# Gated attention and a square-plus MLP on one core: another order of some 1,000 pieces of work, and two of the last four stores issued by ScalarE

## The chip, the cores and the metric

The kernel runs on one core of a Trainium2 chip. Its time is the device time of one execution in microseconds. A core has five engines with an instruction queue each: TensorE (PE, with a weight load PEld ahead of each matmul), VectorE (DVE), ScalarE (ACT), GpSimd (POOL) and SyncE (SP), and 16 DMA engines that all DMAs share, whichever engine issues them. Each engine works through its own queue in order; semaphores order the engines among each other.

## The reference

Inputs `q`, `k`, `v`, `f_logit` have the shape (4, 8, 768, 48): 4 batches, 8 heads, 768 tokens, 48 channels. `w_in` is 384 x 2048 and `w_out` 2048 x 384, all fp32.

```python
f = 1.0 / (1.0 + np.exp(-f_logit))
for t in range(S):
    state = f[:, :, t, :, None] * state + np.einsum('bhd,bhe->bhde', k[:, :, t], v[:, :, t])
    y[:, :, t] = np.einsum('bhd,bhde->bhe', q[:, :, t], state)
...
x = y.transpose(0, 2, 1, 3).reshape(B * S, H * D)      # 3072 x 384
h = x @ w_in
g = 0.5 * (h + np.sqrt(h * h + 4.0))
return (g @ w_out).astype(np.float32)                  # 3072 x 384
```

## The kernel before

**Strips.** The 3072 tokens are cut into 12 strips of 256 tokens, p = 0 to 11; three strips make a batch, so strips 0, 3, 6 and 9 begin with an empty state. A strip is two chunks of 128 tokens (cc = 0, 1). The recurrence is done in blocks: within a chunk as a masked product of scaled q and k, between chunks through a state that is handed on. Strip 0 is loaded and prepared in two halves of four heads (`FINE = [0]`), the others whole.

**Pieces.** `describe` makes a table of named pieces of work; each is a function that emits a few instructions. Nothing is emitted there. The string `ORDER` lists all pieces, one word each, `name:engine` with the PSUM banks behind `@`, and the kernel's last loop walks through it and emits them. The place in the string is the place in that engine's queue: D is VectorE, P is POOL, A ScalarE, S SP, T TensorE. So each engine's queue is written out by hand (or by a program that wrote the string), and an instruction whose input is late holds everything listed behind it on its engine. `cost`, `lock`, `mode` and the like in the table belong to the program that finds an order; the chip doesn't see them.

**The pieces of a strip p**, by the names in the string:
- `lf`, `lk`, `lq`, `lv`: the loads of f, k, q, v, fp32, issued by SP (L174), each into one of three buffers, so that strip p waits until strip p-3 has used its own.
- `ex` (exp of -f, ACT), `ut` (adds 1, DVE), `tt` (product of a pair of tokens), `ln` (ACT), `hi` and `lo` (the logarithm split in two fp16 parts), `cu` (its running sum, on PE), `c1` (DVE), `ep` and `ea` (exp of plus and minus the sum, ACT), `ge`, `gs`, `gb` (the chunk's decay factors).
- `qu`, `ku`, `qm`, `km`: q and k scaled with these; most are on POOL, at 1 and 2 us each.
- `tp` and `te` (strips 0 to 3: transposes of the scaled q and k on PE, copied out of PSUM) or `tx` (strips 4 to 11: DMA transposes, two for a strip, issued by SP, L373).
- `vc`: v cast to fp16. `sc`: scores on PE (L414), `pm`: the mask (DVE). `kv`: the chunk's own state (L442); `ia`, `sp`, `sa`, `sb`: the state added, scaled and handed on. `yt` and `yn`: y from inside the chunk and from the state (L492, L501); `yc`: y copied out of PSUM.
- `xp` and `xe` (strips 0 to 3) or `xx` (strips 4 to 11, a DMA transpose issued by SP, L516): x transposed for the MLP.
- `m1.p.0` to `m1.p.7`: h, six matmuls of 256 columns each (L541); `sq` (square, ACT, L550), `rt` (square root of a pair, ACT, L556), `gt` (g, DVE, L566).
- `m2.p.00` to `m2.p.13`: the output of chunk cc in four quarters (L578), four matmuls of 384 columns each; a quarter n needs the weights `wo`n. `ev`: copied out of PSUM into one of two output buffers `os` (DVE or ACT). `st`: the stores, two for a strip, one for each half of the partitions; for strip 11, whose output leaves chunk by chunk (`SPLIT_OUT`), four. All are issued by SP (L598). `ev` of strip p waits until both stores of strip p-2 have landed.
- `wi0` to `wi3`, `wo0` to `wo3`: the weights of the MLP, in four parts each, issued by POOL with a cast to fp16 (L148, L153). `m1.p.m` needs `wi`(m // 2).
- `TABLE:e` and `TABLE:s` load ScalarE's table for exp and logarithm or for the square root.

The order is a software pipeline: the MLP of strips p-1 and p-2 fills PE while strip p's attention is prepared on the other engines. Around the start, the loads of strips 0 and 1 and the chain `ex`, `ut`, `tt`, `ln`, `hi`, `lo`, `cu` stand first. At the end only the MLP of strips 8 to 11 is left. The end of the string:

```python
m2.10.03:T gt11.6:D m2.11.02:T ev10.0:D m2.11.10:T@5 st10.01.1:S m2.11.11:T st10.01.0:S m2.11.03:T m2.11.12:T ev11.0:D
m2.11.13:T st11.0.0:S st11.0.1:S ev11.1:A st11.1.0:S st11.1.1:S
```

and SP's words around strip 10's transposes, without the other engines':

```python
xx8:S st5.01.0:S tx10.0:S st5.01.1:S tx10.1:S tx11.0:S xx9:S tx11.1:S st6.01.0:S
```

Of the kernel before, what the change touches and what calls it, by code (L numbers as in the profile page):

```python
# [28 lines left out]
DEPTH = {'f': 3, 'q': 3, 'k': 3, 'v': 3, 'UT': 3, 's': 2, 'ep': 2, 'ea': 2, 'v16': 4, 'ge': 3, 'gs': 4, 'gb': 3, 'qkT0': 2, 'qkT1': 2, 'pm00': 2, 'pm01': 2, 'pm10': 2, 'pm11': 2, 'st0': 1, 'pc': 4, 'st1': 1, 'sn0': 2, 'sn1': 2, 'y16': 2, 'xT': 5, 'hsq': 3, 'r16': 3, 'g': 4, 'os': 2}  # L29

ORDER = """
lf0.1:S lf0.0:S lf1.0:S lk0.0:S lk0.1:S TABLE:e ex0.1:A lq0.1:S ut0.1:D ex0.0:A lq0.0:S tt0.1:P ut0.0:D ln0.1:A tt0.0:D
hi0.1:A ln0.0:A lf2.0:S lo0.1:P hi0.0:A ex1.0:A lo0.0:D lv0.0:S cu0.0:T@01 ku0.0:D ut1.0:D cu0.1:T@01 lk1.0:S ku0.1:D tt1.0:D
ep0.1:A qu0.1:D ln1.0:A km0.1:D ea0.1:A ep0.0:A lq1.0:S qm0.1:D ea0.0:A hi1.0:A qu0.0:D tp0.1:T@12 lf3.0:S km0.0:D ex2.0:A
qm0.0:D ge0:A te0.0.1:A ut2.0:D gs0:P lv0.1:S tp0.0:T@12 tt2.0:D lo1.0:P te0.0.0:A te0.1.0:D ln2.0:A lf4.0:S te0.1.1:D hi2.0:A
ku1.0:D sc0.0:T@01 wi0:P sc0.1:T@23 cu1.0:T@45 wi2:P lv1.0:S qu1.0:D ex3.0:A pm0.01:D lk2.0:S lo2.0:P ea1.0:A pm0.10:D vc0.1:A
vc0.0:P cu2.0:T@15 pm0.00:D lq2.0:S ge1:A qm1.0:P ep1.0:A pm0.11:D kv0:T@02 ge2:A ex4.0:A yt0:T@34 sa0:D km1.0:D yn0.1:T
yc0.0:A gb1:P ia0.1:T yc0.1:A xp0.0:T@0 xe0.0:A xp0.1:T@3 ut3.0:D tp1.0:T@46 wi1:P xe0.1:A sb0:D ep2.0:A m1.0.1:T@0 tt3.0:P
ea2.0:A te1.1.0:D m1.0.0:T@7 sq0.1:A wi3:P te1.0.0:D ln3.0:A lf5.0:S ut4.0:D sc1.0:T@12 gs1:P sq0.0:A sc1.1:T@34 pm1.00:D
m1.0.4:T@5 TABLE:s rt0.0:A vc1.0:P pm1.11:D m1.0.5:T@1 tt4.0:P pm1.01:D kv1:T@46 gs2:P ia1.0:T pm1.10:D gb2:P hi3.0:P sq0.5:A  # L40
lv2.0:S gt0.0:D yt1:T@23 ku2.0:P sq0.4:A yn1.0:T sa1:D m1.0.3:T@7 rt0.2:A yc1.0:D ia1.1:T m1.0.2:T@4 gt0.1:D sq0.3:A lo3.0:P
yn1.1:T sb1:D xp1.0:T@0 sq0.2:A km2.0:D wo1:P rt0.1:A cu3.0:T@2 lk3.0:S m1.0.6:T@6 qu2.0:P yc1.1:D TABLE:e ln4.0:A c13.0:D
xp1.1:T@3 lq4.0:S qm2.0:P xe1.1:D xe1.0:D m1.0.7:T@3 gt0.5:D ex5.0:A m1.1.1:T@0 gt0.2:D lq3.0:S ea3.0:A vc2.0:P gt0.4:D
tp2.0:T@14 ge3:A sq0.7:A wo0:P ut5.0:D m1.1.3:T@5 sq1.1:A te2.1.0:D tt5.0:P sq0.6:A te2.0.0:D ep3.0:A wo2:P ln5.0:A lk4.0:S
gt0.3:D sc2.0:T@41 TABLE:s rt0.3:A hi4.0:P pm2.01:D kv2:T@27 wo3:P ia2.0:T pm2.00:D m1.1.0:T@1 lo4.0:P sa2:D m1.1.2:T@4
lf6.0:S sq1.3:A gt0.7:D ku3.0:P ia2.1:T sc2.1:T@27 sq1.2:A gt0.6:D m1.1.5:T@3 rt1.1:A pm2.10:D m1.1.4:T@6 hi5.0:P pm2.11:D
sq1.0:A m2.0.00:T@2 km3.0:P gt1.3:D rt1.0:A m2.0.01:T gt1.2:D yt2:T@57 sq1.4:A yn2.0:T gt1.0:D yn2.1:T qu4.0:P sq1.5:A
m1.1.7:T@4 yc2.1:D rt1.2:A m1.1.6:T@1 lo5.0:P gt1.1:D lf7.0:S cu4.0:T@7 qu3.0:D sq1.6:A gs3:P m2.0.10:T@0 sq1.7:A yc2.0:D
qm3.0:P m2.0.11:T rt1.3:A gt1.4:D xp2.0:T@5 m2.0.02:T lk5.0:S gt1.5:D TABLE:e ep4.0:A cu5.0:T@6 gt1.7:D ku4.0:P xp2.1:T@3
m2.0.12:T xe2.0:D lv3.0:S c15.0:D tp3.0:T@45 ex6.0:A c14.0:D m2.0.03:T km4.0:P xe2.1:D ep5.0:A lf8.0:S te3.0.0:D m2.0.13:T  # L50
ge5:A ex7.0:A te3.1.0:D m1.2.2:T@6 ge4:A lv4.0:S ev0.0:A ut7.0:D sc3.1:T@73 sc3.0:T@45 ea5.0:A m2.1.10:T@2 ut6.0:D tt7.0:P
ev0.1:A lq5.0:S gt1.6:D m2.1.11:T ea4.0:A sq2.2:A tt6.0:D m2.1.12:T qm4.0:P vc3.0:A m1.2.0:T@0 pm3.10:D m2.1.13:T ln6.0:A
pm3.00:D sq2.0:A m1.2.3:T@1 pm3.11:D ln7.0:A gb4:P kv3:T@47 tx4.0:S ku5.0:D hi6.0:P sq2.3:A m2.1.00:T@3 TABLE:s rt2.1:A sa3:D
m2.1.01:T st0.01.0:S km5.0:P sp3.1:D tx4.1:S m1.2.1:T@4 pm3.01:D m2.1.02:T ev1.1:D lv5.0:S yt3:T@57 sq2.1:A lo6.0:D qu5.0:P
lq6.0:S yn3.1:T rt2.0:A gt2.3:D m1.2.5:T@2 gt2.2:D m2.1.03:T qm5.0:P yc3.1:A m1.2.4:T@1 gt2.1:D yc3.0:A lk6.0:S ev1.0:A
sc4.1:T@56 gt2.0:D sq2.4:A sc4.0:T@47 m1.2.6:T@3 pm4.11:D sb3:P sq2.5:A lf9.0:S xp3.1:T@0 pm4.00:D rt2.2:A m1.2.7:T@6 vc4.0:P
pm4.01:D m2.2.10:T@4 sq2.7:A st1.01.1:S st0.01.1:S gs4:P gt2.4:D hi7.0:P m2.2.11:T sq2.6:A qu6.0:P gt2.5:D xp3.0:T@7 cu6.0:T@1
rt2.3:A tx5.0:S pm4.10:D m2.2.12:T lo7.0:P TABLE:e ex8.0:A xe3.1:D yt4:T@25 gt2.7:D ku6.0:P yn4.0:T tx5.1:S m2.2.00:T@0
xe3.0:D gt2.6:D kv4:T@67 lq8.0:S c16.0:D ex9.0:A cu7.0:T@3 vc5.0:P sp4.0:D m2.2.01:T ea6.0:A ut8.0:D ep7.0:A m2.2.13:T lk7.0:S
sa4:D tt8.0:P ge6:A yc4.0:A m1.3.0:T@6 c17.0:D ep6.0:A yn4.1:T ev2.1:D m2.2.02:T ea7.0:A gb5:P ut9.0:D gs5:P ln8.0:A  # L60
m1.3.1:T@4 ge7:A yc4.1:D kv5:T@12 sq3.0:A tt9.0:P sp4.1:D sc5.1:T@23 xx4:S sq3.1:A m2.2.03:T pm5.11:D sb4:P ln9.0:A sc5.0:T@57
pm5.10:D TABLE:s rt3.0:A lv8.0:S m1.3.3:T@3 km6.0:P pm5.01:D lq7.0:S m1.3.5:T@2 sp5.0:D m1.3.4:T@7 lv6.0:S ev2.0:D m1.3.2:T@1
sa5:P pm5.00:D sq3.4:A sq3.5:A gt3.1:D yt5:T@05 hi9.0:P st1.01.0:S rt3.2:A yn5.0:T qm6.0:P yn5.1:T m1.4.1:T@4 yc5.0:D sq3.3:A
gt3.5:D m1.3.7:T@0 sq3.2:A gt3.0:D m1.3.6:T@2 lo9.0:P tx6.0:S rt3.1:A gt3.4:D m1.4.3:T@6 vc6.0:P yc5.1:D sq3.7:A m1.4.4:T@7
lv7.0:S gt3.3:D sq3.6:A qu7.0:P m2.3.10:T@5 tx6.1:S rt3.3:A gt3.2:D m1.4.0:T@3 hi8.0:P gs6:D m2.3.11:T lv9.0:S ku7.0:P sq4.1:A
gt3.6:D m2.3.12:T sq4.0:A gt3.7:D kv6:T@12 rt4.0:A lf10.0:S m1.4.2:T@0 sa6:D vc8.0:P sq4.4:A gt4.0:D m2.3.13:T km7.0:P sq4.3:A
m2.3.00:T@1 sp6.1:D xx5:S sq4.2:A gt4.1:D m1.4.6:T@2 rt4.1:A ev3.1:D m1.4.7:T@3 qu8.0:P lk8.0:S sc6.1:T@45 sq4.6:A gt4.3:D
m2.3.01:T gb7:P sq4.7:A pm6.10:D vc7.0:P m1.4.5:T@6 rt4.3:A lf11.0:S pm6.11:D lo8.0:P m2.3.02:T gt4.2:D sq4.5:A sc6.0:T@45
st2.01.0:S st2.01.1:S qm7.0:P m2.3.03:T rt4.2:A gt4.6:D cu8.0:T@0 pm6.00:D TABLE:e ex10.0:A cu9.0:T@2 gt4.7:D m1.5.3:T@4 sb6:P
tx7.0:S gt4.5:D m2.4.10:T@3 ku8.0:P gt4.4:D m2.4.00:T@6 tx7.1:S ge9:A ge8:A ev3.0:D ep9.0:A m2.4.11:T c18.0:D ex11.0:A lq9.0:S  # L70
m2.4.01:T ut10.0:D gs7:P ea8.0:A m2.4.12:T ut11.0:D ep8.0:A lk9.0:S m1.5.2:T@1 sq5.3:A pm6.01:D tt11.0:P m2.4.13:T sq5.2:A
c19.0:D tt10.0:P yt6:T@05 ev4.1:D ea9.0:A lv10.0:S kv7:T@27 yc6.0:D ln11.0:A yn6.1:T gb8:P m2.4.02:T sp7.0:D ln10.0:A TABLE:s
rt5.1:A yc6.1:D sc7.0:T@03 sa7:P m2.4.03:T pm7.00:D xx6:S qm8.0:P m1.5.1:T@2 sp7.1:D m1.5.0:T@0 ev4.0:D st3.01.0:S sq5.1:A
st3.01.1:S gt5.3:D m1.5.4:T@5 st4.01.1:S sq5.0:A qu9.0:P gt5.2:D m1.5.5:T@6 lq11.0:S rt5.0:A sc7.1:T@47 pm7.01:D hi11.0:P
m1.5.7:T@1 sb7:P sq5.5:A gt5.0:D m1.5.6:T@3 sq5.4:A gt5.1:D hi10.0:P m1.6.2:T@0 rt5.2:A pm7.11:D lo11.0:P m2.5.10:T@2 gs8:D
sq5.7:A m2.5.11:T km8.0:P gt5.4:D sq5.6:A m1.6.0:T@7 gt5.5:D rt5.3:A m1.6.3:T@5 pm7.10:D m2.5.12:T gs9:P sq6.2:A tx8.1:S
# [50 lines left out]
def describe(nc, W, ctx_tiles, aps):  # L127
# [28 lines left out]
    for p in range(NP):  # L156
# [9 lines left out]
        for x, (h0, h1) in enumerate(parts):  # L166
            hs = slice(h0, h1)
            nh = h1 - h0
            for s in "fqkv":
                def load(e, bk, s=s, x=x, hs=hs, p=p):  # L170
                    if (s, p) not in T:
                        T[s, p] = sb(s, p, [128, 8, 2, 48], FP32)
# [556 lines left out]
```

## Time and profile before

| what | value |
|---|---|
| median of 5 runs | 194.56 us (193.85 to 198.29) |
| the profiled execution | 194.52 us, of which the span of its instructions 192.3 us |
| first matmul, end of the last matmul | 6.37 us, 187.9 us |
| clock granted to TensorE | 0.999 over the span; the record of the full clock begins at 21.4 us |
| `gt`, DVE L566, 96 times | 684 ns each |
| `sq`, ACT L550, 96 times; `rt`, ACT L556, 48 times | 592 and 1057 ns each |
| loads of 384 KB, from issue to landing (median) | 5.7 us |
| stores of 192 KB; of 96 KB | 3.1 us; 2.2 us |
| weights of the MLP, from issue to landing | 8.2 us |
| DMA transposes of q and k; of y | 4.4 us; 4.5 us |
| HBM read, written | 25.17 MB, 4.72 MB |

The page gives for each engine the time in which it was busy. PE's matmuls are pipelined and their ends are modelled: six matmuls of L541 in a row start 109 ns apart, though each is listed with 273 ns. So PE's work is better read from the starts of its pieces. The digit rows cut the span into 40 slices of 4.8 us. In a timeline's row stand the start, the time, the engine and line, the operation with output and input, how many instructions were merged, and in brackets the idle time of the engine before it and who ended that.

### The profile page before, as it was taken

To read this page: it belongs to the slowest core of one execution; us is meant where nothing else is said; L and a number is where in the kernel's file an instruction comes from. 1 tells how busy PE (TensorE), PEld (TensorE's weight loads), DVE (VectorE), ACT (ScalarE), POOL (GpSimd) and SP (SyncE) were. 2 spreads that over 40 slices of the span, in tenths; PEclk is the share of its full clock that TensorE was granted. 3 is DMA by queue.
4 is the path that set the end of the run, shared out by engine and by line. 5 is a ranking of instruction groups with operands and counts; after the bars stand their busy time and mean duration, and the time that the engine had idled before them with its cause. 6 is when DMAs were issued, how large, how long until landed. Compare 5 with 4: busy or idle time off the path is not lost.

```text
span 192.3 us, 5596 instructions
## 1 busy us (share of the span) xinstructions
PE 170.2 (89%) x2287; PEld 123.7 (64%) x2287; DVE 149.0 (77%) x280; ACT 153.1 (80%) x246; POOL 117.5 (61%) x146
## 2 busy tenths in 40 slices
PE   0348997779999999998999999999969999999990
PEld 0235876557667766875667876877747688767660
DVE  5696899987989999877999869667759787536640
ACT  4585899898979998899789989987565599896600
POOL 5149689998899599949988996669931000000000
PEclk9999999999999999999999999999999999999999
DMA  5999999999999999999999979990797233000523
GB/s 150 273 258 235 248 218 253 256 219 234 250 220 153 270 182 220 254 189 256 206 178 263 242 112 194 234 177 0 67 142 138 51 78 82 3 0 8 159 75 89
DMA packets 80505, 32.87 MB, mean 171 GB/s; under 512 B 73824, under 2 KB 80480, under 8 KB 80480
## 3 DMA queue, kind: packets, MB, share of 16 engines
q1 hardware_dynamic: 76768, 29.37, 75.0%
q0 software_dynamic: 3712, 3.15, 10.2%
q8 instruction: 18, 0.29, 0.6%
q14 instruction: 7, 0.06, 0.1%
HBM read 25.17 MB, written 4.72 MB: 155 GB/s over the span
## 4 chain that ended last, share of the span: by engine, by line
PE 50%; POOL 18%; DMA 17%; issue 4%; ACT 3%; DVE 3%; SPq 2%; DVEq 0%; POOLq 0%
PE ps L578 23%; PE ps L541 20%; POOL qk L142 6%; DMA qkT<-qk 5%; DMA v<-in_v_dram 5%; DMA wout<-in_moe_w_out_dram 4%; DMA k<-in_k_dram 3%; POOL UT L142 2%; PE ps L414 2%; POOL k L142 2%; PE ps L492 2%; POOL q L142 2%; PE ps L501 1%; POOL hl L266 1%; POOL v L139 1%
## 5 line engine op out<-in xcount | busy, mean ns | idle before, releaser
L566 DVE SCALAR_TENSOR_TENSOR g<-ps,r 128x512 f16<-128x512 f32 x96 | 62.4, 684 | 18.4 <-ACT r L556 18.3
L541 PE MATMUL ps<-xT,win 128*128 128x256 f16 x576 | 72.4, 273 | 2.9 <-ACT os L137 1.3
L578 PE MATMUL ps<-wout,g 128*128 128x384 f16 x384 | 71.2, 326 | 0.5 <-DMA wout<-in_moe_w_out_dram 0.5
L550 ACT ACTIVATE hsq<-ps 128x512 f16<-128x512 f32 x96 | 53.7, 592 | 15.6 <-PE ps L541 15.1
L541 PEld LDWEIGHTS <-win 128*128 128x128 f16 x576 | 55.0, 98 | 14.1 <-issue 3.0
L556 ACT ACTIVATE r<-hsq 128x1024 f16<-128x1024 f16 x48 | 50.6, 1057 | 1.2
L578 PEld LDWEIGHTS <-g 128*128 128x128 f16 x384 | 36.0, 98 | 20.3 <-DMA wout<-in_moe_w_out_dram 0.8
L429 DVE TENSOR_TENSOR pm<-ps,mask 128x512 f16<-128x512 f32 x48 | 30.9, 682 | 4.5 <-PE ps L414 4.3
L142 POOL TENSOR_TENSOR qk<-q,ea 128x384 f16<-128x384 f32 x22 | 22.0, 1023 | 1.3 <-DVE q L142 0.8
L142 POOL TENSOR_TENSOR k<-k,UT 128x768 f32<-128x768 f32 x9 | 16.3, 1816 | 2.3 <-DMA k<-in_k_dram 2.3
L142 POOL TENSOR_TENSOR qk<-k,ep 128x384 f16<-128x384 f32 x18 | 17.6, 997 | 0.1
L283 PE MATMUL ps<-hl,tri 128*128 128x384 f16 (+1 forms) x34 | 9.1, 376 | 7.3 <-ACT hl L258 6.4
L181 ACT ACTIVATE f<-f 128x768 f32<-128x768 f32 (+1 forms) x13 | 10.3, 793 | 3.8 <-DMA f<-in_f_logit_dram 3.6
L414 PE MATMUL ps<-qkT 48*64 48x128 f16 x384 | 9.7, 228 | 2.9 <-DMA qkT<-qk 1.1
L139 POOL CAST v<-v 128x768 f16<-128x768 f32 (+1 forms) x11 | 9.1, 824 | 5.1 <-DMA v<-in_v_dram 5.1
L142 POOL TENSOR_TENSOR q<-q,UT 128x384 f32<-128x384 f32 x9 | 9.0, 999 | 4.1 <-DMA q<-in_q_dram 2.2
L142 POOL TENSOR_TENSOR UT<-UT 128x384 f32<-128x384 f32 (+1 forms) x9 | 9.1, 1016 | 3.8 <-DVE UT L231 3.7
L137 ACT COPY os<-ps 128x384 f32<-128x384 f32 x9 | 4.3, 480 | 8.8 <-PE ps L578 5.0
L414 PEld LDWEIGHTS <-qkT 48*64 48x64 f16 x384 | 6.7, 110 | 7.1 <-issue 3.2
L266 POOL TENSOR_TENSOR hl<-s,hl 128x384 f16<-128x384 f32 (+1 forms) x11 | 10.1, 917 | 0.8 <-ACT hl L258 0.7
L139 DVE CAST y<-ps 128x384 f16<-128x384 f32 x17 | 9.3, 550 | 1.5 <-PE ps L501 1.5
L139 DVE COPY os<-ps 128x384 f32<-128x384 f32 x15 | 8.2, 549 | 2.3 <-PE ps L578 2.3
(71 smaller groups left out, 181.9 us busy)
## 6 DMA issues: line engine op xcount, KB each, us to landing
f<-in_f_logit_dram SPq DMA_DIRECT2D x11, 384.0 KB, 5.7
k<-in_k_dram SPq DMA_DIRECT2D x11, 384.0 KB, 5.7
q<-in_q_dram SPq DMA_DIRECT2D x11, 384.0 KB, 5.8
v<-in_v_dram SPq DMA_DIRECT2D x11, 384.0 KB, 5.8
out_dram<-os SPq DMA_DIRECT2D x22, 192.0 KB, 3.1
win<-in_moe_w_in_dram POOLq DMA_DIRECT2D x4, 384.0 KB, 8.2
wout<-in_moe_w_out_dram POOLq DMA_DIRECT2D x4, 384.0 KB, 8.1
f<-in_f_logit_dram SPq DMA_DIRECT2D x2, 192.0 KB, 2.7
```

The lines of the kernel that those rows point to most:

```text
L139: eng(e).tensor_copy(out=o, in_=i)
L142: eng(e).tensor_tensor(out=o, in0=a, in1=b, op=ALU.mult)
L181: nc.scalar.activation(out=t, in_=t, func=AF.Exp, scale=-1.0)
L266: eng(e).tensor_tensor(out=hl[:, 1, hs, 0:D], in0=T["s", p][:, hs], in1=hl[:, 0, hs, 0:D], op=ALU.subtract)
L283: nc.tensor.matmul(out=T["cum", p, m][:, h0 * D:h1 * D], lhsT=tri[:, m], rhs=t[:, hs, 0:D], start=(r == 0), stop=(r == len(terms) - 1), sk ...
L414: nc.tensor.matmul(out=T["sc", p, i, h][64 * cc:64 * cc + 64, j, :], lhsT=t[r, 1, j, i, :], rhs=t[r, 0, j], start=True, stop=True)
L429: eng(e).tensor_tensor(out=T["pm", p, i, h], in0=T["pc", p, i, h] if key in PMACT else T["sc", p, i, h], in1=K["mask"][:, i].unsqueeze(1). ...
L541: nc.tensor.matmul(out=T["h", p, m][:, a], lhsT=K["win"][m // 2][:, j, m % 2 * 256 + a * 128:m % 2 * 256 + a * 128 + 128], rhs=T["xT", p][ ...
L550: nc.scalar.activation(out=T["hsq", p, r][:, a], in_=T["h", p, m].rearrange("p a c t -> p (a c t)"), func=AF.Square, scale=1.0)
L556: nc.scalar.activation(out=T["r16", p, r], in_=T["hsq", p, r], func=AF.Sqrt, scale=0.25, bias=1.0)
L566: nc.vector.scalar_tensor_tensor(out=T["g", p][:, 2 * m:2 * m + 2, :].rearrange("p a t -> p (a t)"), in0=T["h", p, m].rearrange("p a c t - ...
L578: nc.tensor.matmul(out=T["o", p, cc], lhsT=T["g", p][:, jn, cc * 128:(cc + 1) * 128], rhs=K["wout"][jn // 4][:, jn % 4, :], start=(jn == 0 ...
```

## The change

The string `ORDER` is replaced. Both strings hold the same pieces. Some of them move to another engine:

| pieces | from | to |
|---|---|---|
| `hi3`, `hi6` | POOL | ACT |
| `hi5`, `lo1`, `lo2`, `lo11`, `qm1`, `qu5`, `qu6`, `qu10`, `sa7`, `gs4`, `gs11`, `tt0.1`, `tt7` | POOL | DVE |
| `km2`, `ku1`, `ku5`, `lo6`, `qu3`, `tt2`, `tt6`, `gs6`, `gs8` | DVE | POOL |
| `vc3` | ACT | POOL |
| `vc0.0` | POOL | ACT |
| `te0.1.1`, `te1.0.0`, `xe3.1`, `yc9.0`, `yc10.0`, `ev1.1`, `ev5.0`, `ev7.1`, `ev9.1` | DVE | ACT |
| `xe0.1`, `yc3.1`, `yc7.0`, `yc10.1`, `ev1.0`, `ev6.0`, `ev6.1`, `ev9.0` | ACT | DVE |
| `st11.0.0`, `st11.1.1` | SP | ACT |

The rest keeps its engine and changes its place, mostly by a few words. PE's order is much the same (the sequence of strips and stages stays); PSUM banks are dealt out anew. The words at the start, SP's around strip 10, and the end:

```diff
-lf0.1:S lf0.0:S lf1.0:S lk0.0:S lk0.1:S TABLE:e ex0.1:A lq0.1:S ut0.1:D ex0.0:A lq0.0:S tt0.1:P ut0.0:D ln0.1:A tt0.0:D
+lf0.0:S lf0.1:S lf1.0:S lk0.0:S lk0.1:S TABLE:e ex0.0:A lq0.0:S ut0.0:D ex0.1:A tt0.0:D lq0.1:S ut0.1:D ln0.0:A tt0.1:D
...
-m2.10.03:T gt11.6:D m2.11.02:T ev10.0:D m2.11.10:T@5 st10.01.1:S m2.11.11:T st10.01.0:S m2.11.03:T m2.11.12:T ev11.0:D
-m2.11.13:T st11.0.0:S st11.0.1:S ev11.1:A st11.1.0:S st11.1.1:S
+m2.11.10:T@2 rt11.3:A m2.11.01:T gt11.6:D m2.11.02:T gt11.7:D m2.10.13:T m2.11.03:T ev10.1:D m2.11.11:T ev11.0:D m2.11.12:T
+st11.0.0:A st11.0.1:S m2.11.13:T st10.01.0:S st10.01.1:S ev11.1:A st11.1.1:A st11.1.0:S
```

Queues taken out of the two strings, before (first line) and after (second):

```
SP, loads after lf2:      lv0.0 lk1 lq1 lf3 lv0.1 lf4 lv1 lk2 lq2 lf5 lv2 lk3 lq4 lq3 lk4 lf6 lf7 lk5 lv3 lf8 lv4 lq5 tx4.0
                          lf3 lk1 lv0.1 lf4 lv0.0 lq1 lv1 lk2 lq2 lf5 lv2 lq3 lk3 lk4 lq4 lf7 lf6 lv3 lv4 lv5 lk5 lq5 lk6 tx4.1
POOL, with the weights:   lo1 wi0 wi2 lo2 vc0.0 qm1 gb1 wi1 tt3 wi3 gs1 vc1 tt4 gs2 gb2 hi3 ku2 lo3 wo1 qu2 qm2 vc2 wo0 tt5 wo2 hi4 wo3
                          tt2 ku1 wi0 gs0 tt3 wi2 gb1 gs1 wi1 wi3 vc1 tt4 ku2 lo3 km2 wo0 gs2 gb2 qu2 qm2 wo1 wo2 vc2 tt5 gs3 qu3 qm3 hi4 wo3
SP, strips 4 to 6:        lf9 st1.1 st0.1 tx5.0 tx5.1 lq8 lk7 xx4 lv8 lq7 lv6 st1.0 tx6.0 lv7 tx6.1
                          st1.0 st0.0 lf9 st0.1 tx5.1 tx5.0 lk8 lv6 lq7 xx4 lf11 lk7 st1.1 tx6.0 tx6.1
SP, strips 8 to 11:       xx8 st5.0 tx10.0 st5.1 tx10.1 tx11.0 xx9 tx11.1 st6.0
                          st5.0 st5.1 xx8 tx10.1 tx10.0 tx11.0 xx9 tx11.1 st6.1
POOL, strips 5 and 6:     ku6 vc5 tt8 gb5 gs5 tt9 sb4 km6 sa5 hi9 qm6 lo9 vc6
                          ku6 tt8 tt9 qm6 gb5 sb4 gs5 hi8 sa5 km6 vc6 hi9 gs6
```

(`st5.0` is short for the word `st5.01.0` and so on.) The stores of strip 11 may be put on ACT, an unused way to load v straight to fp16 is added (no strip is in `VDMA`), and an unused word for extra matmuls goes:

```diff
+VDMA = []
...
-            for s in "fqkv":
+            for s in ("fqk" if p in VDMA else "fqkv"):
...
+            if p in VDMA:
+                def vd(e, bk, x=x, hs=hs, p=p):
...
+                    nc.gpsimd.dma_start(out=T["v16", p][:, hs].rearrange("p h i d -> p h (i d)"),
+                                        in_=v[bb][hs, t0:t0 + 256, :].rearrange("h (p i) d -> p h (i d)", i=2))
...
-                W.add(f"st{p}.{''.join(map(str, cs))}.{i}", "SP" if p in SPLIT_OUT else "S", st, reads=[f"os{p}.{c}" for c in cs], makes=[],
-                      uses=[("os", p)], dma=("o", 0.28 * len(cs)), cost={"S": 0.5, "P": 0.8})
+                W.add(f"st{p}.{''.join(map(str, cs))}.{i}", "SPA" if p in SPLIT_OUT else "S", st, reads=[f"os{p}.{c}" for c in cs], makes=[],
+                      uses=[("os", p)], dma=("o", 0.28 * len(cs)), cost={"S": 0.6, "P": 0.8, "A": 0.6})
...
-            if name.startswith("wm"):
-                t = ps(banks, [128, 128], FP32)
-                for n in range(int(name[2:])):
-                    nc.tensor.matmul(out=t, lhsT=ident, rhs=ident, start=True, stop=True)
-                continue
```

## The prediction

> **What bounds the kernel now.** I read the page first, then the chain of waits in time order, then the instruction timeline of the stretches where the chain leaves TensorE, then the last microseconds.
>
> ```profile
> span 192.3 us, 5596 instructions
> PE 170.2 (89%) x2287; PEld 123.7 (64%) x2287; DVE 149.0 (77%) x280; ACT 153.1 (80%) x246; POOL 117.5 (61%) x146
> ...
> PE   0348997779999999998999999999969999999990
> ...
> POOL 5149689998899599949988996669931000000000
> ...
> DMA  5999999999999999999999979990797233000523
> ```
>
> Each digit is 4.8 us. DMA is full to about 57 us, POOL nearly so from 24 to 140 us, and PE from 48 us to the end, with one dip at 140 us. So there are three regimes: data decide the first 45 us, then PE's own work decides, while POOL and the transposes decide whether PE meets a hole.
>
> To compare two orders of the same work I add up PE's pieces as they stand in the list, each at its row's full-clock time: the chain has 2.62 us for 24 matmuls of L541, so 0.655 us for an `m1`, and 3.25 us for 20 of L578, so 0.65 us for an `m2`; likewise 0.25 for `sc`, 0.35 for `kv`, 0.5 for `yt`, 0.17 for `yn`, `ia` and `xp`, 0.66 for `tp` (0.33 for a half), 0.53 to 0.85 for `cu`. The sum is 157.7 us in either kernel. A piece's start less the work listed ahead of it is its **lag**: 22.2 - 6.5 = 15.7 us at the first `m1`, 42.1 - 20.4 = 21.7 at the first `m2`, 24.3 at `sc6.1`, 26.8 at `sc9.0`, 27.2 at `kv10`, 29.9 at `sc11.1`, 30.2 at PE's end (187.9). Only lag and tail can change. The largest step in the late part is the 2.7 us from `kv10` to `sc11.1`:
>
> ```profile
> 127.01 0.63 SPq L598 DMA_DIRECT2D out_dram<-os  x1
> 135.36 1.26 SPq L373 DMA_TRANSPOSE qkT<-qk  x1
> 136.67 1.75 SPq L598 DMA_DIRECT2D out_dram<-os  x1
> ...
> 138.52 3.74 SPq L373 DMA_TRANSPOSE qkT<-qk  x2
> ...
> 141.04 0.48 ACT L137 COPY os<-ps 128x384 f32<-128x384 f32 x1 [3.82 <-DMA out_dram<-os]
> ...
> 141.57 0.82 PE L541 MATMUL ps<-xT,win 128*128 128x256 f16 x6 [1.31 <-ACT os L137]
> ...
> 142.91 0.64 PE L414 MATMUL ps<-qkT 48*64 48x128 f16 x31 [0.35 <-DMA qkT<-qk]
> ```
>
> SP issues in list order. `st5.01.1` stands behind `tx10.0`, which waits for POOL until 135.36. Its buffer is free only about 141 us, so `ev7.0` holds ScalarE for 3.82 us and PE for 1.31. The second transpose, behind that store, then holds `sc10` (one matmul at 142.31, the rest at 142.91). By start-to-start times this is 1.47 us over the normal `m2.7.10` and 0.55 over `sc10.1`: **2.0 us**.
>
> **The change, part by part.**
>
> *Engines.* Counting moved pieces: SP 102 to 100, ScalarE 246 to 251 instructions, VectorE 262 to 265, POOL 134 to 128, PE 291 pieces as before. At mean durations ScalarE gains 1.8 us, VectorE 0.1, POOL loses 1.8. ScalarE idles 39 us in the span (192.3 - 153.1), so this is hidden; if it fell on a full stretch it would cost up to 1.8. The `VDMA` list is empty and no `wm` word is in either list: both edits emit nothing, 0.
>
> *Start and weights, 0 to 45 us.* `wi0` now stands on POOL behind `tt2.0` (1.0) and `ku1.0` (1.8, waiting for k1, now one load later): about 15.7 us instead of 13.98, so m1's first weights come 1.7 us later. The `win` transfers run one behind another at some 3.4 us each (8.2 us to landing in the page). I get `m1.0.4` at 26.1 (24.2 before), lag 17.2 against 15.9. In return `wo0` stands earlier, near 29 us (34.60 before), and `vc1.0` no longer waits for v1 until 24.07, since v1 rides ahead of the late weights. `m2.0.00` then starts near 38.3 with 18.5 ahead, and the next `m2`s wait for `wo1` and `wo2` near 40.4 and 43.4: lag 21.5 by 43 us, against 21.7. The late start is paid back: 0. Bounds: -1.5 (only the earlier `wo0` counts) to +2 (the late weights are not made up).
>
> *Strips 3 to 9, 45 to 135 us.* For each transpose I compare the POOL work ahead of it with PE's need. `km6` and `qm6` are both done after 62.6 us of POOL work (61.9 before), and `sa5` ahead of them waits for `kv5`, which moved back by 3.1 us of PE work: tx6 comes some 0.7 us later. But `tx6.1` follows `tx6.0` directly; before, a v load that waited for POOL stood between:
>
> ```profile
> 81.34 2.23 SPq L373 DMA_TRANSPOSE qkT<-qk  x1
> 83.62 0.72 SPq L174 DMA_DIRECT2D v<-in_v_dram  x1
> 84.47 1.46 SPq L373 DMA_TRANSPOSE qkT<-qk  x1
> ```
>
> `sc6.1` stands 1.4 us earlier in PE's list, so its wait (1.05 us over normal before) stays about the same. `km8` comes 4.6 us of POOL work earlier, `km9` 3.8 later with `tx9.0` still in time. I take 0; bounds -1.05 (that wait gone) to +1.5 (tx6 and tx9 each late by their 0.7).
>
> *Strips 10 and 11, 127 to 152 us.* `st5.01.0` and `st5.01.1` now stand together ahead of `xx8` and both tx10, so `ev7.0` finds its buffer. `km10` and `qm10` end after 105.8 us of POOL work, not 109.0; the two tx10 are adjacent and near 132 us. Both holes go: **-2.0**. What is late next: `xx9` stands behind `tx11.0`, which waits for `km11`, and that for `sa10` on POOL, which needs `kv10` (about 137 us). I get `km11` at 140.9, `xx9` at 142.2, landed 4.5 us later at 146.7, while `m1.9.1`, now with 119.1 us of work ahead, wants it at 146.1: **+0.6**. Bounds 0 (yc9 first) and +1.5 (a transpose at 5.97, as tx6.1 in the chain).
>
> *The tail.* Two of strip 11's four stores go to ScalarE's queue.
>
> ```profile
> 184.78 4.87 SPq L598 DMA_DIRECT2D out_dram<-os  x6
> ...
> 187.94 0.48 ACT L137 COPY os<-ps 128x384 f32<-128x384 f32 x1 [4.98 <-PE ps L578]
> ```
>
> Before, the last two issues follow one another on SP after ACT's copy (188.42): 188.46 and 189.06, 0.55 and 0.59 us. Now they go out together, 0.6 saved. An issue on ScalarE is not in this trace: nearest rows are SP's 0.50 to 0.59 and POOL's 0.80; I take 0.6, SP's, as the queues use the same form. `st11.0.0` on ScalarE stands ahead of `ev11.1`, issued about 1.3 us before PE ends, so it is done in time. But both strip-10 stores now stand behind `st11.0.1` on SP and are issued within the last 0.7 us; four such stores moved in 3.3 us at 177 to 181, so six stores' data crowd the end. I take **-0.4**; bounds -0.6 and +0.2.
>
> The Trainium skill's "DMA: Bandwidth & Descriptors" (Rules for kernel authors) speaks against this part: spreading DMAs over issuing engines does not add bandwidth, and only saves issue time. By the rule alone the sum's tail would be 0 if the crowd of stores sets the end; the row's spacing of 0.6 us, equal to the issue spacing, says that issue set it before, so I keep the saving.
>
> *The clock.* PE's work before about 21 us runs at half rate (four 384-column matmuls of `cu1.0` take 1.46 us; those at 45 us half that), and the order of pieces up to there hardly changes. 0; a grant 2 us earlier or later would be worth about 1 us, as half of what is done meanwhile.
>
> "TensorE: Matmul & The Clock Gate" (What you observe) puts the release near 4 us of sustained matmuls, give or take 0.5; here PE is nearly steady from 13.7 us and the clock came at 21.4. By the page the penalty before it would be shorter, but in both kernels alike.
>
> *Other small waits.* Some 250 pieces on VectorE and ScalarE stand in a new order; PE's holes between 46 and 88 us were 1.6 us before. I add +0.3 for new ones; bounds 0 and 1.6.
>
> **Sum:** 0 + 0 - 2.0 + 0.6 - 0.4 + 0 + 0.3 = -1.5. Span 192.3 - 1.5 = 190.8; the profiled execution took 194.52, 2.2 around its span, and the runs' median is 194.56: **193.0 us**.
>
> **Rivals.**
> - *The holes only move (no change).* Lag is set by POOL and transposes, and a gain at 140 us is eaten by `xx9`, `tx11.1` and strip 6: +0.6 becomes 1.5 and strips 3 to 9 cost 1.0: 193.0 + 0.9 + 1.0 = 194.9. For it: POOL is full in both. Against: POOL has 1.8 us less and `km10` is earlier.
> - *Slower, by one mechanism: SP's queue ahead of strips 5 to 9.* `st1.01.0` now stands ahead of `st0.01.0`, f9 and both tx5, and waits for `ev1`, near 64 us; f9 was issued at 63.61 before. If that is 66 or later, `ex9`, `ut9`, `tt9`, `qm6`, `km6` and tx6 follow on POOL in list order. Every microsecond past the 2 us that `km6` has (it waits for `sa5` anyway) lands on `sc6.1`. It decides once tx6.1 is issued after 86 us: at 88 us +4, total 197.0. For it: POOL's in-order wait of 2.21 us at 66.92 already came from a load. Against: f9's consumers are also listed later.
> - *Clean run (faster still).* The strip 6 wait goes too, `xx9` is in time, the early `wo0` gives its full 1.5, and no new waits come: 193.0 - 1.05 - 0.6 - 1.5 - 0.3 = 189.6.
>
> **How the numbers follow.** Forecast 0.50, holes move 0.19, slower 0.24, clean 0.07. A measurement of this kernel tells about 0.5% (1 us) from no change: faster is under 193.6, slower over 195.5. The forecast's own range is 191.5 to 194.2, a quarter of it not under 193.6. Faster: 0.39 + 0.07 + 0.02 of the mixed case = 0.48; same: 0.11 + 0.12 = 0.23; slower: 0.24 + 0.05 = 0.29. Leaving out the clean end and the worst of the slow case, the range is 190.8 to 197.0.
>
> **What would show it.** Right: no ScalarE wait on `os` from a store near 140 us and no idle before `sc10`; `wi0` issued near 15.7 us and `m2.0.00` near 38; the last two stores issued within 0.1 us; PE's end less 157.7 near 28.7. Wrong: lag above 22.5 at `m2.0.03` (weights not made up), tx6.1 issued after 86 us, or a PE wait of over 1 us before `m1.9.1` or `sc11.1`; a new long wait of ScalarE or VectorE would break the sum altogether.

## The result, and the profile after

| | before | after |
|---|---|---|
| median of the runs | 195.72 us (193.60 to 201.11, 79 runs) | 196.12 us (194.66 to 199.79, 44 runs) |
| ratio after to before, 95% interval | | **1.0066** [1.0048, 1.0085] |
| profiled execution; its span | 194.52; 192.3 us | 195.64; 193.9 us |
| TensorE's first matmul; end of its last | 6.37; 187.91 us | 5.49; 189.31 us |
| from there to the end of the span | 4.4 us | 4.6 us |

The kernel became slower by 0.7%, some 1.3 us; the forecast was 1.5 us less. Ratios here leave out executions that are over 1.5% above the fastest of their kernel, of which the kernel before has many, so a ratio is not the quotient of the two medians beside it.

The head of the page after, for the rows that were shown of before and that of the clock:

```profile
span 193.9 us, 5580 instructions
...
PE 171.0 (88%) x2287; PEld 124.6 (64%) x2287; DVE 151.9 (78%) x283; ACT 154.3 (80%) x249; POOL 114.8 (59%) x140
...
PE   0328599889998999999999999999979999999990
...
POOL 4126899699999976799939969907990100000000
PEclk9999859999999999999999999999999999999999
DMA  5999999999974999799999799995359850201406
```

TensorE has the same 2287 matmuls; GpSimd has 2.7 us less to do. Three things are new: GpSimd stands at 0 in the 27th slice (126 to 131 us), some 15 us ahead of TensorE's one late dip; the clock record shows 8 and 5 in the fifth and sixth slice; and DMA's last three slices carry 4, 0 and 6 where they carried 5, 2 and 3.

The prediction's lag (a piece's start less the TensorE work listed ahead of it), read at three places of that work:

| | before | after |
|---|---|---|
| lag at 24 us of work | 21.8 | 23.6 |
| step from 24 to 112 | 5.4 | 6.0 |
| step from 112 to TensorE's end | 3.0 | 2.0 |
| tail | 4.4 | 4.6 |
| lag and tail, with 157.7 of work | 192.3 | 193.9 |

The late step did shrink, by 1.0 instead of the 1.4 that the sum had. The start costs 1.8 and the middle 0.6, where the sum had 0 and 0.

It is not the weights of the MLP that hold TensorE in the start. The record after shows no wait of TensorE for them (before, one: 0.53 us ahead of `m2.0.00`). From 20 us on it waits for products of VectorE and a factor of ScalarE instead:

```profile
23.92 0.82 PE L400 MATMUL ps<-ident,qk 64*128 64x64 f16 x24 [0.80 <-DVE qk L143]
...
24.96 2.77 PE L551 MATMUL ps<-xT,win 128*128 128x256 f16 x12
...
39.06 0.52 PE L452 MATMUL ps<-v,qk 64*128 64x96 f16 x16 [1.01 <-ACT ge L362]
```

The second row is the first two `m1`, at half clock (last section): 2.77 us, where the first two of before took 1.47.

Now the place where GpSimd stands still. Its timeline after, 124 to 134 us (start, length, line, operation; in brackets the idle time before it and what ended that):

```profile
124.26 1.82 POOL L143 TENSOR_TENSOR k<-k,UT 128x768 f32<-128x768 f32 x1 [0.25 <-DMA k<-in_k_dram]
131.91 1.00 POOL L143 TENSOR_TENSOR q<-q,UT 128x384 f32<-128x384 f32 x1 [5.83 <-DMA q<-in_q_dram]
132.85 0.82 POOL L140 CAST v<-v 128x768 f16<-128x768 f32 x1
133.64 1.95 POOL L143 TENSOR_TENSOR qk<-k,ep 128x384 f16<-128x384 f32 x2
135.54 1.95 POOL L143 TENSOR_TENSOR qk<-q,ea 128x384 f16<-128x384 f32 x2
```

SP's queue in the same stretch:

```profile
124.04 3.23 SPq L383 DMA_TRANSPOSE qkT<-qk  x2
127.32 1.27 SPq L175 DMA_DIRECT2D q<-in_q_dram  x1
128.69 1.28 SPq L608 DMA_DIRECT2D out_dram<-os  x2
130.05 1.29 SPq L526 DMA_TRANSPOSE xT<-y  x1
137.53 7.88 SPq L383 DMA_TRANSPOSE qkT<-qk  x3
```

And TensorE, where it meets the delay:

```profile
141.18 0.82 PE L551 MATMUL ps<-xT,win 128*128 128x256 f16 x6
142.99 0.64 PE L424 MATMUL ps<-qkT 48*64 48x128 f16 x32 [0.99 <-DMA qkT<-qk]
```

These rows make one chain. SP's list has q11's load, `lq11`, behind both transposes of strip 9, and the first of them, `tx9.1`, waits for `km9`, the last product of strip 9 on GpSimd (end 124.0). So the load goes out at 127.32, and `qu11`, which needs it, starts at 131.91. It stands on GpSimd ahead of `km10` and `qm10`: they end at 135.6 and 137.5, and the two tx10 go out at 137.5 and 138.9. `sc10` waits for them. GpSimd waits for a load which waits, in SP's queue, for GpSimd.

### The profile page after: what moved, and what is told of

Same layout as the page of the kernel before. It is cut to its first block, busy times and chain, and to the rows that moved or that the text cites. A ratio compares the mean times of both kernels' runs of the same rounds, so it can differ in the third digit from the quotient of the medians.

```text
span 193.9 us, 5580 instructions
## 1 busy us (share of the span) xinstructions
PE 171.0 (88%) x2287; PEld 124.6 (64%) x2287; DVE 151.9 (78%) x283; ACT 154.3 (80%) x249; POOL 114.8 (59%) x140
## 4 chain that ended last, share of the span: by engine, by line
PE 69%; DMA 9%; DVE 9%; ACT 6%; issue 2%; SPq 2%
PE ps L551 29%; PE ps L588 27%; PE ps L424 3%; DMA q<-in_q_dram 3%; PE ps L502 2%; DVE qk L143 2%; DMA f<-in_f_logit_dram 2%; DMA qkT<-qk 2%; PE ps L452 2%; SPq L175 2%; PE ps L511 2%; DMA xT<-y 2%; PE ps L284 1%; DVE g L576 1%; ACT f L182 1%
## 5 line engine op out<-in xcount | busy, mean ns | idle before, releaser
L551 PE MATMUL ps<-xT,win 128*128 128x256 f16 x576 | 73.7, 276 | 0.5 <-DMA xT<-y 0.5
L143 POOL TENSOR_TENSOR qk<-q,ea 128x384 f16<-128x384 f32 x20 | 19.9, 1015 | 0.3
L143 POOL TENSOR_TENSOR k<-k,UT 128x768 f32<-128x768 f32 x11 | 19.9, 1810 | 0.3 <-DMA k<-in_k_dram 0.2
L143 POOL TENSOR_TENSOR qk<-k,ep 128x384 f16<-128x384 f32 x20 | 19.5, 997 | 0.5 <-ACT ep L313 0.3
L143 POOL TENSOR_TENSOR UT<-UT 128x384 f32<-128x384 f32 x9 | 9.5, 1058 | 16.4 <-DVE UT L232 16.4
L140 POOL CAST v<-v 128x768 f16<-128x768 f32 x11 | 9.9, 898 | 1.7 <-DMA v<-in_v_dram 1.7
L143 POOL TENSOR_TENSOR q<-q,UT 128x384 f32<-128x384 f32 x7 | 7.0, 998 | 5.8 <-DMA q<-in_q_dram 5.8
L267 POOL TENSOR_TENSOR hl<-s,hl 128x384 f16<-128x384 f32 (+1 forms) x9 | 8.1, 905 | 3.6 <-ACT s L249 3.2
```

The source lines that it names most:

```text
L140: eng(e).tensor_copy(out=o, in_=i)
L143: eng(e).tensor_tensor(out=o, in0=a, in1=b, op=ALU.mult)
L267: eng(e).tensor_tensor(out=hl[:, 1, hs, 0:D], in0=T["s", p][:, hs], in1=hl[:, 0, hs, 0:D], op=ALU.subtract)
L551: nc.tensor.matmul(out=T["h", p, m][:, a], lhsT=K["win"][m // 2][:, j, m % 2 * 256 + a * 128:m % 2 * 256 + a * 128 + 128], rhs=T["xT", p][ ...
```

## The experiments

In the diffs, a line is a stretch of the order list, cut to the words of one queue.

**q11's load taken out from behind tx9** (the changed kernel otherwise):

```diff
 SP:
-tx8.0 lq10 st4.1 ... tx9.1 tx9.0 lq11 st5.0 st5.1
+tx8.0 lq10 lq11 st4.1 ... tx9.1 tx9.0 st5.0 st5.1
```

> The changed kernel with one load moved: q11's load stands on SP's queue right behind q10's (behind tx8.0) instead of behind tx9.0. Theory A (GpSimd's pace, with the loads it waits for, sets when tx10 and tx11 come): GpSimd's 5.8 us of idle time before qu11 goes, km11 and tx11 come 4 to 5 us earlier, sc10's 1.15 us wait for tx10 goes, and the ratio to the kernel before falls from 1.0066 to 0.998 to 1.002. Rival B (the loss is TensorE's lag of the first 25 us): 1.005 to 1.008, whatever GpSimd does.

Measured: 194.89 us (12 runs), ratio to before **0.9978** [0.9943, 1.0014]. GpSimd's and TensorE's timelines of this run (its line numbers are one lower):

```profile
125.60 1.82 POOL L142 TENSOR_TENSOR k<-k,UT 128x768 f32<-128x768 f32 x1 [0.42 <-DMA k<-in_k_dram]
127.38 0.99 POOL L142 TENSOR_TENSOR q<-q,UT 128x384 f32<-128x384 f32 x1
...
133.77 0.20 POOL L142 TENSOR_TENSOR gb<-gs,ge 128x8 f32<-128x8 f32 x1
138.07 0.83 POOL L142 TENSOR_TENSOR sn<-st,gb 128x384 f16<-128x384 f32 x1 [4.10 <-PE ps L587]
```

```profile
142.24 0.82 PE L550 MATMUL ps<-xT,win 128*128 128x256 f16 x6
142.99 0.64 PE L423 MATMUL ps<-qkT 48*64 48x128 f16 x32
```

The 5.8 us are gone, the tx10 go out at 133.5 and 134.9, four microseconds earlier, and `sc10` follows without a wait. Theory A holds, with the ratio at the lower edge of its range, and the whole loss against the kernel before is gone. The changed kernel with only its last two stores given back to SP (below) was measured beside it and has 1.0096, so the gain is not one between two occasions. Its size is less sure than its sign: the record of this run, of an execution of 195.9 us, is no shorter than that of the changed kernel (194.1 and 193.9 us); its lag is 24.2 at 24 us of work (23.6 there), and from 110 to 114 us of work it grows by 0.2 instead of 1.3. One part of the expectation failed: `km11` and tx11 came no earlier (144.6, before this edit 144.1), since GpSimd now waits 4.1 us for TensorE ahead of `sb9`.

**Two more loads earlier.**

```diff
 SP, besides:
-lf11 ... lq8 ... lf10 ... lv9
+lf11 lf10 ... lq8 lv9 ...
```

> As the run with q11's load moved, with f10's load also right behind f11's and v9's right behind q8's on SP, so that GpSimd's 2.9 us before tt11 and 1.7 us before vc9 go too. Theory A: ratio to the kernel before 0.994 to 1.000, below that of the run with q11's load alone. Rival B: 1.004 to 1.008.

Measured: 197.00 us (12 runs), **1.0095** [1.0050, 1.0141]: the expectation failed. In its profile the lag stays below that of the changed kernel up to 64 us of work and then jumps by 3.5 us, from 27.0 to 30.5, where `sc6.1` waits 1.45 us for its transpose and the next three MLP pieces run 0.5 to 0.6 us over. These three are the clock's: it stands at half from 92.9 to 96.3 us. SP's queue had tx6 at 84.0 us in the changed kernel and at 84.9 here, behind more loads. A load that is moved up sits ahead of something else. Which part of the 1.0095 that is, and which the clock's, this one record does not tell.

**The same kind of edit on the kernel before.**

```diff
 SP (kernel before):
-lv10 ... lq10 ... lk10 ... lq11 ... lv11 ... st5.0 tx10.0 st5.1
+lv10 lq10 lk10 ... lq11 lv11 ... st5.0 st5.1 tx10.0
```

> The kernel before with st5.01.1 right behind st5.01.0, the loads of q10 and k10 right behind v10's, and v11's right behind q11's. Theory A (GpSimd's waits for loads, and the store that holds ev7.0, set the late lag): GpSimd's idle times before qu10, ku11 and vc11 go, tx10 and tx11 come about 2 us earlier, ratio to the kernel before 0.988 to 0.995. Rival (the path from 112 us of content on is TensorE's alone): 0.996 to 1.002, as with the store moved alone (0.998).

Measured: 201.06 us (6 runs, five of them at 200.3 us or more, the fastest 197.23); no ratio was formed. In its record GpSimd's wait for k11's load ahead of `ku11` is 5.65 us, up from 1.57. The expectation failed, and the run is no measure of the waits that it meant to take away.

**The two halves crossed.** Two kernels take one of the two orders for the first 50 us (to `tp3.0`) and the other behind it; a third adds matmuls to the start of the changed kernel:

```diff
 "old, then new":  before's first 268 words, then the rest in the order of after
 "new, then old":  after's first 270 words, then the rest in the order of before
 "more matmuls":   after, +51 matmuls of 128 columns, behind cu0.1, tp0.1, tp0.0, yt0, xp0.0, xp0.1
```

> The order of before up to about 50 us (268 words), then the changed order. Theory: the changed kernel loses in its first 50 us (TensorE's lag is 1.75 us larger there, half of it at half clock) and gains a little later: ratio to before 0.995 to 0.999. Rival (the loss is made after 50 us): ratio 1.006 or more.

Measured, old then new: 198.06 us (6 runs), **1.0112** [1.0040, 1.0184].

> The changed order up to about 50 us (270 words), then the order of before. Theory (loss in the first 50 us): the lag of 1.75 us is carried to the end, ratio 1.007 to 1.010. Rival (loss later): 0.998 to 1.002.

Measured, new then old: 195.75 us (12 runs), **0.9982** [0.9937, 1.0028].

> The changed kernel with 51 matmuls of 128 columns on a free bank in TensorE's idle stretches before 23 us (24 behind cu0.1, 8 behind tp0.1, 9 behind tp0.0, 6 behind yt0, 2 behind each xp0), so that the clock has no idle stretch to fall back on. If the second stretch at half clock (23.1 to 29.9 us in the profile) is what costs the 1.75 us of lag: clock near 1.0 in all runs, ratio to before 0.997 to 1.000. If weights, DVE and POOL set the pace there anyway: the clock is granted, but the ratio stays at 1.004 to 1.007.

Measured, with 51 more matmuls in TensorE's holes of the first 25 us: 196.84 us (12 runs), **1.0058** [1.0016, 1.0101]. Neither case's condition came: the mean clock was 0.962 to 0.991 in its twelve runs, not near 1. So the run does not tell what the half clock costs.

The loss goes with the late order, not with the start, though it is at the start that the lag is made. In its record "old, then new" has the smaller lag at 20 us of work (22.0 against 23.5). It loses this lead at `m1.4.1`, the first piece that needs strip 4's DMA transpose (in the changed kernel TensorE waits 0.51 us there):

```profile
82.75 1.48 PE L550 MATMUL ps<-xT,win 128*128 128x256 f16 x12 [1.76 <-DMA xT<-y]
```

and falls behind where the changed kernel lost time too:

```profile
POOL q L142 <- DMA q<-in_q_dram: 6.8, 1, 6.8
...
PEld L423 <- DMA qkT<-qk: 2.7, 1, 2.7
```

These are its waits from 120 to 160 us (total, times, longest). GpSimd waits 6.8 us for q11's load instead of 5.8, and TensorE, which is no earlier any more (the `m1` ahead of `sc10` starts at 141.26, in the changed kernel at 141.18), idles 2.42 us in front of `sc10` instead of 0.99.

**The store of strip 5 alone.** The kernel before, with `st5.1` ahead of tx10:

```diff
 SP (kernel before):
-st5.0 tx10.0 st5.1 tx10.1
+st5.0 st5.1 tx10.0 tx10.1
```

> The kernel before with one word moved: st5.01.1 stands on SP right behind st5.01.0, ahead of xx8 and tx10, instead of behind tx10.0. Theory of the prediction: the two holes of PE near 140 us (1.47 and 0.55 us over normal) both come from this place, so 2.0 us go: ratio to before 0.990. Rival (lag is set by POOL and the transposes, the holes only move): ratio 0.997 to 1.000, with a new wait of 1 us or more before sc10, m1.9 or sc11.

Measured: 197.44 us (12 runs), 0.9977 [0.9914, 1.0040]: too wide to tell. (The word stands behind `xx8`, as in the diff, not ahead of it as the expectation says.) So the same edit was tried in "new, then old", with ScalarE's two last stores:

> The new order for the first 50 us, then the order of the kernel before with st5.01.1 right behind st5.01.0 and the last stores by ScalarE. The prediction's price for the store's move is 2.0 us and for ScalarE's store 0.4 us: if both come through, 2 us less than that mixture without them (0.9982), ratio 0.985 to 0.990. Rival (the wait for ev7.0 only covers the next one, for GpSimd's pace): 0.994 to 0.999.

Measured: 193.98 us (12 runs), 0.9962 [0.9921, 1.0002]: in the rival's range, but without its pair measured beside it.

> The mixture of the new order up to 50 us and the old order behind it, last stores by ScalarE, with st5.01.1 left where the kernel before has it (behind tx10.0). By the prediction's price the store's place costs 2.0 us, so this run is 1.5 to 2.0 us slower than the same mixture with the store moved (of this call); by the rival (the wait only covers GpSimd's) within 0.5 us of it. ScalarE's wait of 3 to 4 us for st5.01.1 near 140 us is there, and 1 to 2.3 us of lag between 112 and 116 us of content.

Measured, store not moved: 195.75 us (12 runs), 1.0001 [0.9955, 1.0046].

> The same mixture with st5.01.1 right behind st5.01.0, once more, as the measure for the run beside it: ratio to the kernel before 0.992 to 1.000.

Measured beside it, store moved: 195.04 us (12 runs), **0.9942** [0.9893, 0.9991]. So the move is worth about 0.6%, 1.1 us, between the two expectations, and the intervals overlap. ScalarE's waits from 120 to 160 us in the run without it, and then with it (the earlier of the two):

```profile
ACT os L137 <- DMA out_dram<-os: 3.8, 1, 3.8
```

```profile
ACT os L137 <- PE ps L587: 1.8, 1, 1.8
```

The wait on the store goes. Lag from 112 us of work to the end is 2.8 without the move and 1.7 with it: 1.1 us as well. The rest of the predicted 2.0 stays, since tx10 goes out at 137.1 and 138.5, and `sc10` still waits 0.42 us for it.

**The last two stores.** First the changed kernel with ScalarE's two given back to SP, then the kernel before with two given to ScalarE:

```diff
-st11.0.0:A st11.1.1:A
+st11.0.0:S st11.1.1:S
```

> The changed kernel with the two last stores that ScalarE issues given back to SP. As the prediction had it, ScalarE's issue saves 0.4 us, so this run is 0.4 to 0.6 us slower than the changed kernel (ratio to the kernel before 1.008 to 1.010). Rival (the stores of strip 10 crowd the end, and who issues the last one decides nothing): within 0.2 us of the changed kernel, 1.005 to 1.008, with 4.4 to 4.8 us between TensorE's last matmul and the end of the span.

Measured: 197.06 us (12 runs), 1.0096 [1.0044, 1.0149]; TensorE's end 189.87, span 194.9, tail 5.0 us. The tail is that of the first case, 0.4 above the changed kernel; the ratio cannot tell the two apart.

> The kernel before with nothing changed but the issuer of two last stores: ScalarE issues st11.0.0 and st11.1.1, as in the change. The prediction priced this part at 0.4 us of gain (bounds 0.2 of loss to 0.6 of gain): ratio 0.996 to 0.999, with some 4.0 us between TensorE's last matmul and the end of the span instead of 4.4. Rival (the last packets set the end, whoever issues): 4.4 us, ratio 0.999 to 1.002.

Measured: 195.81 us (12 runs), 1.0028 [0.9983, 1.0073]; TensorE's end 191.67, span 195.7, tail 4.0 us. ScalarE's timeline at its end:

```profile
190.99 0.55 ACTq L607 DMA_DIRECT2D out_dram<-os  x1
191.70 0.48 ACT L137 COPY os<-ps 128x384 f32<-128x384 f32 x1 [4.98 <-PE ps L587]
192.21 0.50 ACTq L607 DMA_DIRECT2D out_dram<-os  x1
```

The tail in the records is shorter by 0.4 us in both pairs (4.4 to 4.0, 5.0 to 4.6), and in the mixtures above it is 4.4 with SP's stores ("new, then old") and 4.1 with ScalarE's. The second run's ratio lies above both ranges and does not show it: 0.4 us are 0.2%, and the interval reaches 0.45% to either side.

**Strip 10's stores out of the end.** With q11's load moved, and:

```diff
 TensorE: -m2.10.12 m2.11.00 m2.11.10 m2.11.01 m2.11.02 m2.10.13   +m2.10.12 m2.10.13 m2.11.00 ...
 SP:      -st11.0.1 st10.0 st10.1 st11.1.0                         +st10.0 st10.1 st11.0.1 st11.1.0
```

> The changed kernel with q11's load moved and the end of strip 10 taken forward: m2.10.13 right behind m2.10.12, ev10.1 behind it, and both stores of strip 10 behind m2.11.00, ahead of strip 11's on SP. If the crowd of strip 10's stores at the end holds the tail at 4.6 us, it falls to 3.9 to 4.2 us and the ratio to the kernel before is 0.994 to 0.997; if the last store's own path (0.5 us of ev11.1, 0.55 of issue, 2 of transfer and the rest) sets it, 4.5 to 4.6 us and 0.997 to 1.000.

Measured: 195.01 us (12 runs), **1.0001** [0.9964, 1.0039]; tail 4.1 us. SP's last issues after, and in this run:

```profile
187.99 2.46 SPq L608 DMA_DIRECT2D out_dram<-os  x4
```

```profile
184.64 5.74 SPq L607 DMA_DIRECT2D out_dram<-os  x4
```

Four stores go out within 2.46 us in the one and over 5.74 us in the other. The tail fell from 4.6 to 4.1 as the first case had it; the ratio lies outside its 0.994 to 0.997. The changed kernel ran beside it:

> The changed kernel itself once more, beside the versions of this call. Theory A (q11's load behind tx9.0 on SP makes the loss): some 1.2 us (0.6 per cent) slower than the version of the earlier call with q11's load moved, as far as two calls can be compared, and ratio to the kernel before 1.004 to 1.009. Rival (that difference was the spread between calls): 0.996 to 1.002.

Measured: 196.28 us (12 runs), **1.0091** [1.0055, 1.0127]. So, side by side, the moved load and the tail together are worth 0.9%, no more than the load had alone: the 0.5 us of the tail show in the records, not in the time.

**GpSimd's work ahead of sb9**, on top of the last version:

```diff
 GpSimd: -gb11 sb9 qm11 vc11 sa10 km11   +gb11 qm11 vc11 km11 sb9 sa10
```

> As the run with the end of strip 10 taken forward, with qm11, vc11 and km11 ahead of sb9 on GpSimd, so that they fill its 4.1 us of waiting for TensorE: tx11 comes some 4 us earlier. If tx11 still holds anything (kv11 and yn10 lost 0.5 us), 0.3 to 0.5 us less than the run without it, ratio 0.991 to 0.996; if TensorE has other work by then, the same time within 0.2 us.

Measured: 194.34 us (12 runs), 0.9988 [0.9959, 1.0017]. tx11 starts at 136.3 instead of 144.4. The ratio moves by 0.1%, well inside the intervals, and the step from 112 us of work to TensorE's end is 1.1 us against 1.2: nothing there that a measurement tells, as the second case had it.

**Is the early lag still paid when the load is repaired?** That version again, and the same with the old start:

> The version with q11's load moved, GpSimd's work ahead of sb9 and strip 10's stores taken forward, once more, as the measure for the two others of this call: ratio to the kernel before 0.996 to 1.001.

Measured: 194.29 us (12 runs), 0.9973 [0.9941, 1.0005].

> The order of the kernel before for the first 50 us, then that of the repaired version (q11's load behind q10's, GpSimd's work ahead of sb9, strip 10's stores forward). Theory A (TensorE's lag of the first 50 us is absorbed or given back, and the loss was q11's load): within 0.5 per cent of the repaired version, on either side. Rival B (the early lag of the new order, 0.9 to 1.8 us, is still paid at the end and was covered only by other waits): 0.9 to 1.8 us faster than the repaired version, ratio 0.988 to 0.993.

Measured: 196.32 us (12 runs), 1.0027 [0.9975, 1.0080]. The old start is not faster: rival B wanted 0.988 to 0.993 and falls, and the 0.54% between the two lie just past the 0.5% of theory A. Of the lag this says less than it was meant to. The one record of this version, of an execution of 197.83 us at a mean clock of 0.979, has a lag of 26.5 at 24 us of work, and TensorE waits 1.6 us for strip 4's transpose, as in "old, then new": the mixture has a wait of its own that may eat an earlier start.

**What is best.** New start, old order behind it, store moved, ScalarE's stores: 0.9962 and 0.9942. Only the second interval lies wholly below 1. It is the one version with a sign of beating both kernels, by some 0.5% over the kernel before.

## Why the prediction was wrong

The sum was -1.5 us and +1.3 came. By its own steps:

- **The step that failed: strips 3 to 9, "`km9` 3.8 later with `tx9.0` still in time. I take 0", and the tx10 "adjacent and near 132 us".** `km9` ended at 124.0 against 115.9, 8 us later and not 3.8. I asked only whether `tx9.0` still met TensorE's need, and it did. What stands behind it on SP was not asked: `lq11`, 3.3 us later, then 4.6 us until `qu11` had its data, then `km10` and `qm10` in order on GpSimd. The tx10 came at 137.5 and 138.9. With the load moved they came at 133.5 and 134.9, and the time fell by 0.9% (1.0066 to 0.9978), 1.7 of the 2.8 us by which the forecast missed (the two intervals together allow some 0.9 to 2.5). GpSimd's work ahead of `km10` had been counted (105.8 us), its waits had not: 5.83 us for q11's load, and ahead of `km9` 2.9 for VectorE at `tt11` and 1.7 for v9's load.
- **The late holes, -2.0: right place, too large a size.** `ev7.0` no longer waits for the store (shown by the waits above), but the move alone is worth 1.1 us, with GpSimd's pace as the next limit. With the load repaired too, the step from 112 us of work to TensorE's end is 1.2 us, against 3.0 before: -1.8, most of the price.
- **`m1.9.1` waiting for `xx9`, +0.6: did not come.** TensorE shows no wait there after. But `xx9` went out at 145.50 instead of 142.2, and TensorE came to `m1.9.1` at 150.35 instead of 146.1, so the term was not met as it was priced: both were late.
- **Start and weights, 0.** `wi0` was issued at 15.95 (predicted 15.7), but `m1.0.4` came at 29.7 (26.1) and `m2.0.00` at 41.9 (38.3). The lag at 24 us of work was 1.8 us larger than before, over the 22.5 that the prediction had named as a sign of being wrong. But its reason, weights not made up, is not what the record shows: TensorE did not wait for weights. The estimate followed the weights alone, and VectorE, ScalarE and the clock held TensorE longer. Part is the clock (below): the version with sb9 moved, profiled at a mean clock of 0.998, has +0.9. What makes the other 0.9 stays open. The crossed runs show that this lag alone does not decide the end, as "new, then old" is no slower than before and the old start is no faster with the repaired rest. What I had not seen is that lags of TensorE need not add up to the end: in "old, then new" the early lead went into one longer wait, at `m1.4.1`.
- **The tail, -0.4: the saving was right, the sum was not.** ScalarE's issues take 0.51 to 0.54 us, the last two go out 0.03 us apart, and 0.4 us are saved in both pairs of records. But the two strip 10 stores behind `st11.0.1`, named in the prediction and priced only in the upper bound (+0.2), cost about 0.5: tail 4.6 with them at the end, 4.1 without.
- **Engines, 0, and the rivals.** GpSimd's lighter load brought nothing, since it waited longer instead. "Slower by SP's queue" had the right kind of mechanism, a load late on SP that holds GpSimd, at the wrong place: f9 went out at 67.63, past the 66 that it named, and yet `sc6.1` shows no wait after. "The holes only move" had the right pace-setters, GpSimd and the transposes, but the gain at 140 us was eaten at `sc10`, not by `xx9`, `tx11.1` or strip 6. The clean run did not come.
- **A slip in the signs.** "PE's end less 157.7 near 28.7" takes the tail's -0.4 off TensorE's end as well; the sum gives 29.1 there. It was 31.6.

What stays open: the 1.1 us of the miss that the moved load does not give back (0.9978 is 0.4 us under the kernel before, the forecast was 1.5 under), and how it is shared between the start, the middle and the tail; how much of the start's +0.9 to +1.8 us would be paid in an order without any later wait that covers it, and which part of the 0.6 us in the middle is the order's. Single records of one and the same kernel differ by 2 us in span (193.9 and 196.2, the second at a mean clock of 0.944), so steps under 1 us from one record are not settled by it.

## What to carry to other kernels

When an order is changed, follow every queue behind a wait that moves, not only the consumer of the piece that waits: here a transpose that was still in time held a load, and the load held the engine that feeds the transposes. Look for such rings, in which an engine waits for a load that stands in a queue behind that engine's own product. And do not add up the delays of one engine as if nothing behind them could cover them: cross the halves of the two orders first, which told here where the loss was made better than the lag did, and look for waits that the mixture itself brings in. An early estimate that follows one input alone (here the weights) needs a look at the other engines that feed the same piece.

## What the hardware showed

The clock fell back early in the profiled execution after. Stretches of 3.4 us, first after, then before (length; busy time of PE, PEld, DVE, ACT and POOL, with instructions; granted clock; DMA share; GB/s):

```profile
19.70:23.10 3.40, 1.80 (x62) 1.33 (x56) 3.37 (x7) 2.60 (x9) 3.37 (x6) 1.00 1.17 250
23.10:26.50 3.40, 2.60 (x35) 1.90 (x34) 2.65 (x5) 1.02 (x2) 2.16 (x3) 0.50 1.24 228
26.50:29.90 3.40, 3.40 (x56) 2.29 (x55) 1.55 (x3) 3.10 (x5) 3.40 (x4) 0.50 1.20 206
```

```profile
19.70:23.10 3.40, 3.30 (x72) 2.68 (x66) 3.11 (x7) 2.62 (x7) 2.07 (x3) 1.00 1.18 230
23.10:26.50 3.40, 3.40 (x68) 2.42 (x66) 3.36 (x6) 3.37 (x5) 2.92 (x7) 1.00 1.20 234
```

After, a stretch with TensorE busy for 1.80 of 3.40 us is followed by two at half clock; before, with 3.30, by none. The run with 51 more matmuls shows a fall-back too: full from 14.6 to 18.0 us with 2.16 us busy, then half from 18.0 to 21.4. So the clock came 5 us earlier and was lost again, and these matmuls gained nothing. But the busy time alone does not decide it, since later in the same run as little busy time is followed by the full clock:

```profile
28.26:31.67 3.41, 2.08 (x45) 1.67 (x46) 2.23 (x4) 2.06 (x3) 3.39 (x6) 1.00 1.19 226
```

Nor is the fall-back the change's own. The kernel before with nothing changed but the issuer of two last stores, or the place of strip 5's store, has in its record 6.8 us at half clock between 29 and 40 us, and the changed kernel with its stores given back to SP has none. One and the same order, the version with sb9 moved, was profiled twice: once without a fall-back (mean clock 0.998), once with two (0.982). The prediction's clock term was 0, for a grant that comes once and stays.
